# BigBird attention and a Fourier mixing layer on one core: table loads moved behind their copies, and the last output tiles in another order

## The chip, the cores and the metric

The kernel runs on one core of one Trainium2 chip. The metric is the device time of one execution in microseconds (us). The median of three runs of the kernel before is 1051.01 us (1050.29 to 1051.64).

## The reference

The inputs are `q`, `k`, `v` of shape (4, 8, 768, 64): 4 batches, 8 heads, 768 positions, head size 64. A block mask (blocks of 32: the window, first and last blocks, three sampled blocks for each row of blocks) is applied to the scores.

```python
scores = q @ k.T / sqrt(64); scores = where(mask, scores, -1e9)
x = softmax(scores) @ v                      # heads joined: (4, 768, 512)
mixed = real(fft(fft(x, axis=1), axis=2))
u = x + mixed
un = (u - mean(u)) / sqrt(var(u) + 1e-6)
out = u + relu(un @ w_ch1) @ w_ch2           # w_ch1 (512, 2048), w_ch2 (2048, 512)
```

## The kernel before

**Slots.** The attention is cut into 96 slots, and `slot(sl)` (line 1433) writes out the instructions of one of them on all engines, in a fixed order. Twelve units make a pair of heads, two units a slot, six slots a pair, and 24 slots a batch. A slot begins on PE (the tensor engine) with eight score matmuls (`s<-qT,kT`, L578). ACT (the scalar engine) takes their exponentials (`e<-s`, L598), PE adds up the products with v (`o<-e,vr`, L652) and, in the first batch, the sums (`sp`, L723). The score tile `s` has two buffers, so the scores of a slot wait for the exponentials of the slot before. In the trace slots 8 to 14 begin on PE at 44.49, 49.65, 54.18, 58.76, 63.91, 70.42 and 76.57 us.

**Weights.** Beside the first batch, the two weight matrices come in as 32 chunks of 512 KB, as pairs of 32-bit words, and are turned into floats. `w_load(i)` (line 454) issues the load of chunk i on SP's queue, into one of five rooms in turn; so chunk i has to wait until the round of chunk i-5 is over. `w_round(i)` (line 459) is the round of a chunk: two ACT instructions (L465, L468), then five on DVE, the vector engine (L469 to L477), whose last, L477, ends the use of the room. At the end of a slot `w_loads()` issues the loads that the rounds of earlier slots have made room for, and `w_steps(sl)` writes the rounds: after slot sl, 1.42 times sl of them, rounded up. Slot 8 ends with rounds 10 and 11, slot 9 with round 12, slot 10 with 13 and 14, slot 11 with 15, slot 12 with 16 and 17.

**Tables.** The cosines and sines of the transform go through two buffers `raw` (tag `tr`, called `tab` in the trace). `table_s` (line 383) and `table_d` (line 404) return two functions each: `get` issues the loads on SP's queue (L391, or L409 and L410), and `put` copies the table out of the buffer on DVE (L397, L414 to L421). `table_step()` (line 429) is the last call of the even slots from slot 4 on. Once two loads are out, it runs the oldest `put` and then the next `get`, in the same slot. So the six tables are loaded in slots 4, 6, 8, 10, 12, 14 and copied in slots 8, 10, 12, 14, 16, 18, and from slot 8 to 14 the load follows the copy that frees its buffer. The transform of the first batch, which reads the tables, starts after slot 24.

**SP's queue.** SP (the sync engine) issues almost all transfers, one after another, in the order in which they are written. When one of them waits for a buffer, all behind it wait too. Behind the table load of slot 8 stand the loads of q for a later pair (`load_q`, line 250: six transfers, slot 9) and chunks 15, 16 and 17.

**Rows.** The positions are kept in an order of their own. `_ORDER` (line 53) lists, for each of the six tiles of 128 rows, the runs of rows in memory; `_rows` (line 80) makes one transfer of each, and joins two runs of 63 that go backwards into one of 126 rows. Tiles 2, 3 and 4 go as 1, 126 and 1 rows, tiles 0 and 1 as 64 and 64, and tile 5 as 1, 63 and 64. `spread_q` (line 287) also walks `_ORDER`, at the start of the kernel.

**The end.** The last batch has an output stage of its own. `outputs(r, m, after)` (line 1210) works for m on tile m (half 0, in xA) and tile 3+m (half 1, in xB) in 28 matmuls of `yy` (L1224), and DVE adds the results to x (L1231, L1254). m runs through `OUT` (line 1178), here (2, 0, 1). `store` (line 1167, issues at L1170) sends a tile to memory. In the last call alone (`ends`) each tile goes in two halves of 256 columns. The order there is: left half of tile m on SP, left half of tile 3+m on ACT's queue, right half of tile 3+m on SP, and, after the last sum, right half of tile m on SP. Behind the last store stands a conditional (L1666) that jumps over a general version of the kernel, and then the closing of the program (L1701).

Of the kernel before, what the change touches and what calls it, by code (L numbers as in the profile page):

```python
# [27 lines left out]
def _run(ap, start, n, step):  # L28

    at = ap[:, start:start + 1]  # L30
    return bass.AP(tensor=at.tensor, offset=at.offset, ap=[list(at.ap[0]), [step, n]])
# [9 lines left out]
def _grid(ap, start, runs, jump, n, step):  # L41
# [16 lines left out]


_TURNED = (((0, 0, (128, 64, 2), (64, 128, 2), (1, 1, 64)),  # L60
# [19 lines left out]
def _rows(view, tile):  # L80

    got = []
    for t, p0, runs, jump, n, s0, step in _ORDER:
        if t != tile:
            continue
        at = view[s0:s0 + 1, :]
        row, col = list(at.ap[0])[0], list(at.ap[1])
        if jump > 0 > step:
            got.append((p0, runs * n, bass.AP(tensor=at.tensor, offset=at.offset,
                                              ap=[[jump * row, runs], [step * row, n], col])))  # L90
            continue
        for r in range(runs):
            at = view[s0 + r * jump:s0 + r * jump + 1, :]
            got.append((p0 + r * n, n, bass.AP(tensor=at.tensor, offset=at.offset,
                                               ap=[[step * row, n], col])))
    return got
# [3 lines left out]
def kernel(  # L100
# [19 lines left out]
    P = 128  # L120
# [262 lines left out]
    def table_s(src, dst, t):  # L383
        raw = tr_p.tile([P, ND * HS], FP32, tag="tr", name="tab")

        def get():
            rows = _rows(src, t)
            if dst is sn_sb and t == 0:
                rows = [(0, 1, src[P:P + 1, :]), (1, 63, src[2:P:2, :]), (64, 64, src[1:P:2, :])]
            for p0, cnt, of in rows:  # L390
                nc.sync.dma_start(out=raw[p0:p0 + cnt, 0:KS], in_=of)  # L391

        def put():
            to = 0
            for s0, n, step in FREQUENCIES:
                if to < dst.shape[2]:
                    nc.vector.tensor_copy(out=dst[:, t, to:to + n], in_=_run(raw, s0, n, step))  # L397
                to += n
        return get, put
# [4 lines left out]
    def table_d(src, dst):  # L404
# [7 lines left out]
        def put():  # L412
# [5 lines left out]
            else:  # L418
# [5 lines left out]
    table_steps = [(table_s, (src, dst, t)) for src, dst in ((cos_s, cs_sb), (sin_s, sn_sb))  # L424
                   for t in range(2)]
    table_steps += [(table_d, (cos_d, cd_sb)), (table_d, (sin_d, sd_sb))]
    table_put = deque()

    def table_step():

        if len(table_put) == 2 or not table_steps:
            if table_put:
                table_put.popleft()()
        if table_steps:
            fn, args = table_steps.pop(0)
            get, put = fn(*args)
            get()
            table_put.append(put)
# [4 lines left out]
    for w, w_sb in ((w_ch1, w1_sb), (w_ch2, w2_sb)):  # L443
        rows, cols = w.shape
        words = _words(w, rows * cols)
        for row in range(rows // P):
            for col in range(0, cols, WN):
                src = bass.AP(tensor=words, offset=2 * (row * P * cols + col),
                              ap=[[2 * cols, P], [1, 2 * WN]])
# [532 lines left out]
    def mixer(b, xA, xB):  # L982
# [184 lines left out]
        def store(half, m, cols=slice(0, DM), queue=nc.sync):  # L1167
            x = (xA, xB)[half]
            for p0, cnt, rows in _rows(out[b][:, cols], T * half + m):
                queue.dma_start(out=rows, in_=x[p0:p0 + cnt, m, cols])  # L1170
            if m == out_of[half][-1]:
                finished.add((b, half))
# [2 lines left out]


        last = b == B - 1
        OUT = (2, 0, 1)
        out_of = (OUT, OUT if last else (0, 1, 2))
        o_t, o_s = {}, {}  # L1180
        DH = DM // 2
# [13 lines left out]
        def output_left(m, j):  # L1195
            a11, a12, a21, a22 = (hs[g, i][:, :, m * P:(m + 1) * P]
                                  for i in range(2) for g in range(2))
            if j in (1, 3):
                o_s[m, j] = ep.tile([P, 4, P], FP32, tag="e", name="os")
            elif j == 4:  # L1200
                o_s[m, j] = acc_p.tile([P, 4, P], FP32, tag="acc", name="os")

            to, a, c, op = {1: (o_s.get((m, 1)), a21, a22, ALU.add),
                            2: (a21, o_s[m, 1], a11, ALU.subtract),
                            3: (o_s.get((m, 3)), a22, a21, ALU.subtract),
                            4: (o_s.get((m, 4)), a12, a21, ALU.subtract)}[j]
            tt(out=to, in0=a, in1=c, op=op)
            busy("DVE", 0.7)

        def outputs(r, m, after):  # L1210

            if m == OUT[0]:
                output_left(m, 1)
# [30 lines left out]
            if ends:  # L1244
                store(0, m, slice(0, DH))
            if m == OUT[0]:
                output_left(m, 3)
# [53 lines left out]
        for r in range(2 if last else 0):  # L1301
            rest += [(lambda p=p: quad(p), 7 * PRODUCT) for p in range(4 * r, 4 * r + 4)]
            rest += [(lambda r=r, m=m, after=after: outputs(r, m, after), 7 * 1.75)
                     for m, after in zip(OUT, OUT[1:] + (None,))]
        for r in range(0 if last else NF // 4):
# [94 lines left out]
    def begin(b):  # L1400


        before, after, rest = mixer(b, x_of[b, 0], x_of[b, 1])
        any_of = len(late) + len(apart) + 4 * len(rest)
        hold = 2 * T
        apart.extend((*step, any_of) for step in norm_steps(b) + before)
        apart.extend((*step, hold) for step in after)

        def go():
            late.extend(rest)  # L1410
        apart.append(("-", go, 0.0, 0.0, 0.0, hold))
# [16 lines left out]
    def w_steps(sl):  # L1428
        while state["w"] < min(len(wchunks), W_PACE * sl):
            w_round(state["w"])  # L1430
            state["w"] += 1

    def slot(sl):
# [126 lines left out]
            item[2]()  # L1560
        w_loads()
        w_steps(sl)
        if sl >= 4 and sl % 2 == 0:
            table_step()

    def highest():

# [24 lines left out]
    for sl in range(B * SB + 1):  # L1592
        slot(sl)
        if sl == B * SB - 4:
            flag = highest()
        if sl == B * SB - 2:
            over = nc.values_load(flag[0:1, 0:1], min_val=0, max_val=1)
# [6 lines left out]
    def general():  # L1604
# [4 lines left out]
        for b in range(B):  # L1609
            xs = [xp.tile([P, T, DM], FP32, tag=tag, name="x") for tag in ("xA", "xB")]  # L1610
            for h in range(H):
# [43 lines left out]
                for half, x in enumerate(xs):  # L1655
                    sl = slice(half * T, half * T + T)
                    nc.vector.tensor_tensor(out=x[:, :, h * D:(h + 1) * D], in0=op[:, sl, :],
                                            in1=rs[:, sl, :].broadcast_to([P, T, D]),
                                            op=ALU.mult)
            before, after, rest = mixer(b, *xs)  # L1660
            for step in before + after:
                step[1]()
# [42 lines left out]
```

## Time and profile before

| what | value |
|---|---|
| median of 3 runs | 1051.01 us (1050.29 to 1051.64) |
| profiled execution | 1051.83 us |
| its span, first to last instruction | 1049.9 us |
| mean granted clock of PE | 0.994 |
| PE idle before the scores of slot 13 | 2.24 us |
| last instruction that computes ends at | 1040.81 us |

The profiled execution took 1.93 us more than its span, and 0.82 us more than the median. All positions are microseconds from the start of the span. In a line of the timeline the first number is the start, the second the length; in brackets is the idle time of the engine before it, and what ended it. A merged line (x5) holds several instructions of one kind. A line of waits has the total, the number and the longest. SPq and ACTq are the two engines as issuers of transfers; q1 and q10 are their transfer queues. In a table by stretches a line has the stretch, its length, the busy time of the five engines, the clock granted to PE, the busy share of the 16 transfer engines and GB/s.

### The profile page before, as it was taken

Reading aid. Unit: us, or ns where it says so; the run is one execution under the profiler, and the core shown is the slowest. Engines: PE = TensorE matmul, PEld = TensorE weight load, DVE = VectorE, ACT = ScalarE, POOL = GpSimd, SP = SyncE. Lnnn points to the kernel's source line nnn. Section 1 sums busy time; section 2 is a strip of 40 time slices with the busy share of each in tenths; the row PEclk is TensorE's granted clock in tenths of the full one; section 3 lists DMA queues with packets and bytes.
Section 4 is the critical chain, followed back from the end, with each engine's and each line's share of the span. In section 5 each row is a group of like instructions: output and inputs, shape, how many; then the busy total and the mean of one; then the engine's idle time right before and its main releaser. Section 6 shows DMA issues by size and latency. Waiting matters only on the chain. (4 is left out here: it accounts for less than half of the span.)

```text
span 1049.9 us, 12342 instructions
## 1 busy us (share of the span) xinstructions
PE 1022.6 (97%) x4350; PEld 530.7 (51%) x4350; DVE 672.5 (64%) x1232; ACT 356.2 (34%) x718; POOL 236.6 (23%) x264
## 2 busy tenths in 40 slices
PE   8999999999999999999999999899999999999996
PEld 4333345444465554444444654444445654578585
DVE  6898885977845844655578467565558364774663
ACT  6979756554020112432441211243221111210210
POOL 1000074655000100554553001256420001000000
PEclk9999999999999999999999999999999999999998
DMA  7757522282000035232220003721010001000001
GB/s 212 227 180 216 121 47 46 51 140 37 1 1 20 31 40 87 62 64 39 56 58 1 1 10 74 124 53 42 16 25 7 0 1 39 22 1 1 1 17 46
DMA packets 163455, 58.05 MB, mean 55 GB/s; under 512 B 144172, under 2 KB 154170, under 8 KB 163386
## 3 DMA queue, kind: packets, MB, share of 16 engines
q1 hardware_dynamic: 162134, 56.45, 24.1%
q10 hardware_dynamic: 1220, 0.72, 0.3%
q8 instruction: 36, 0.59, 0.2%
q14 instruction: 33, 0.27, 0.1%
q0 software_dynamic: 32, 0.01, 0.0%
HBM read 43.80 MB, written 13.37 MB: 54 GB/s over the span
## 5 line engine op out<-in xcount | busy, mean ns | idle before, releaser
L638 POOL TENSOR_TENSOR acc<-acc,e 128x384 f32<-128x384 f32 x156 | 159.2, 1054 | 90.6 <-DVE e L608 68.2
L578 PE MATMUL s<-qT,kT 64*128 64x384 f32 x768 | 154.0, 515 | 9.8 <-ACT e L598 8.4
L652 PE MATMUL o<-e,vr 128*64 128x384 f32 x768 | 142.9, 499 | 0.0
L1159 PE MATMUL y<-w_sb,hB 128*128 128x512 f32 x288 | 128.1, 595 | 0.3 <-DVE x L1162 0.3
L1159 PE MATMUL y<-w_sb,hA 128*128 128x512 f32 x288 | 127.9, 595 | 0.0
L1162 DVE TENSOR_TENSOR x<-y,x 128x512 f32<-128x512 f32 x72 | 49.7, 690 | 113.8 <-PE y L1159 113.4
L608 DVE TENSOR_TENSOR e<-s,mask 128x768 f32<-128x768 f32 x84 | 76.3, 950 | 54.5 <-ACT s L606 46.3
L578 PEld LDWEIGHTS s<-qT,kT 64*128 64x128 f32 x768 | 63.7, 185 | 90.6 <-ACT e L598 29.0
L638 POOL TENSOR_TENSOR acc<-e 128x384 f32<-128x384 f32 x42 | 48.0, 1164 | 249.7 <-ACT e L598 125.6
L606 ACT ACTIVATE s<-s 128x768 f32<-128x768 f32 x84 | 63.6, 792 | 113.9 <-PE s L578 113.7
L598 ACT ACTIVATE e<-s 128x768 f32<-128x768 f32 x108 | 82.6, 812 | 56.0 <-PE s L588 35.0
L1103 PE MATMUL z<-unT,t 128*128 128x384 f32 x256 | 93.5, 488 | 0.0
L1159 PEld LDWEIGHTS y<-w_sb,hB 128*128 128x128 f32 x288 | 53.4, 190 | 66.5 <-issue 65.2
L1159 PEld LDWEIGHTS y<-w_sb,hA 128*128 128x128 f32 x288 | 53.7, 190 | 63.7 <-issue 60.0
L652 PEld LDWEIGHTS o<-e,vr 128*64 128x64 f32 x768 | 48.0, 137 | 69.7 <-issue 67.8
L1108 DVE TENSOR_TENSOR hA<-z,hA 128x384 f32<-128x384 f32 x64 | 35.7, 557 | 71.6 <-PE z L1103 71.5
L1112 ACT ACTIVATE hA<-hA 128x384 f32<-128x384 f32 x64 | 33.4, 523 | 123.6 <-DVE hA L1108 123.6
L1103 PEld LDWEIGHTS z<-unT,t 128*128 128x128 f32 x256 | 49.1, 192 | 34.4 <-issue 0.9
L1112 ACT ACTIVATE hB<-hB 128x384 f32<-128x384 f32 x64 | 33.5, 523 | 88.6 <-DVE hB L1108 88.6
L1123 ACT COPY hA<-xp 128x384 f32<-128x384 f32 x32 | 15.3, 477 | 123.3 <-PE xp L1103 123.3
L1103 PE MATMUL z<-t,w_sb 128*128 128x384 f32 x128 | 46.7, 488 | 2.8 <-DVE t L1065 2.8
L1103 PE MATMUL z<-t,t 128*128 128x384 f32 x128 | 47.8, 497 | 0.0
(208 smaller groups left out, 1372.5 us busy)
## 6 DMA issues: line engine op xcount, KB each, us to landing
wraw<-in_moe_w_ch_dram SPq DMA_DIRECT2D x32, 512.0 KB
vr<-in_v_dram SPq DMA_DIRECT2D x30, 192.0 KB
far<-un SPq DMA_DIRECT2D x18, 256.0 KB
unT<-far SPq DMA_DIRECT2D x24, 192.0 KB
qb<-in_q_dram SPq DMA_DIRECT2D x44, 96.0 KB
kb<-in_k_dram SPq DMA_DIRECT2D x44, 96.0 KB
out_dram<-x SPq DMA_DIRECT2D x11, 252.0 KB
out_dram<-x SPq DMA_DIRECT2D x18, 128.0 KB
```

Source lines behind the costliest of these rows:

```text
L578: nc.tensor.matmul(s[:, i, 0:HS], kT[rows, c * P:(c + 1) * P], qT[rows, queries], start=True, stop=u not in by_pe)
L598: nc.scalar.activation(out=e, in_=s[:, :, 0:HS], func=ACT.Exp, scale=scale)
L606: nc.scalar.activation(out=s[:, :, 0:HS], in_=s[:, :, 0:HS], func=ACT.Exp, scale=scale)
L608: nc.vector.tensor_tensor(out=e, in0=s[:, :, 0:HS], in1=m.broadcast_to([P, 2, HS]), op=ALU.mult)
L638: nc.gpsimd.tensor_add(out=acc[:, i, :], in0=start[:, i, :], in1=e[:, i, :])
L652: nc.tensor.matmul(o[D * i:D * i + D, :], vt[:, i, c, :], e[:, i, :], start=(c == 0), stop=(c == C - 1))
L1103: nc.tensor.matmul(to, a[:, k, :], c[:, k, :], start=(k == 0), stop=(k == ND // 2 - 1))
L1108: tt(out=to, in0=ps, in1=a, op=ALU.add)
L1112: nc.scalar.activation(out=h, in_=h, func=ACT.Relu)
L1123: nc.scalar.copy(out=h11, in_=x)
L1159: nc.tensor.matmul(y, hs[0, half][:, l, m * P:(m + 1) * P], w2_sb[:, 4 * r + l, :], start=(l == 0), stop=(l == 3))
L1162: nc.vector.tensor_tensor(out=x[:, m, :], in0=y, in1=x[:, m, :], op=ALU.add)
```

## The change

There are three edits.

1. `table_step` takes the slot's number and looks it up in a list. Loads stand in slots 4, 5, 11, 12, 17 and 18, copies in slots 8, 9, 14, 15, 20 and 21. The order of the six tables stays, and no slot has both.
2. The run of 63 rows of tile 5 becomes two runs of 48 and 15. This goes for every store of tile 5 (one transfer more each), for one sine load, and for the copies of `spread_q` (one more in each of two calls).
3. In the last batch `OUT` is (0, 1, 2): the last call of `outputs` works on tiles 2 and 5, where it worked on tiles 1 and 4.

```diff
-          (5, 0, 1, 0, 1, 512, 1), (5, 1, 1, 0, 63, 386, 2), (5, 64, 1, 0, 64, 385, 2))
+          (5, 0, 1, 0, 1, 512, 1), (5, 1, 1, 0, 48, 386, 2), (5, 49, 1, 0, 15, 482, 2),
+          (5, 64, 1, 0, 64, 385, 2))
...
-                rows = [(0, 1, src[P:P + 1, :]), (1, 63, src[2:P:2, :]), (64, 64, src[1:P:2, :])]
+                rows = [(0, 1, src[P:P + 1, :]), (1, 48, src[2:98:2, :]),
+                        (49, 15, src[98:P:2, :]), (64, 64, src[1:P:2, :])]
...
-    def table_step():
-
-        if len(table_put) == 2 or not table_steps:
-            if table_put:
-                table_put.popleft()()
-        if table_steps:
+    TABLES = {4: "g", 5: "g", 8: "p", 9: "p", 11: "g", 12: "g", 14: "p", 15: "p",
+              17: "g", 18: "g", 20: "p", 21: "p"}
+
+    def table_step(sl):
+
+        if TABLES.get(sl) == "p":
+            table_put.popleft()()
+        elif sl in TABLES:
             fn, args = table_steps.pop(0)
             get, put = fn(*args)
             get()
...
-        OUT = (2, 0, 1)
+        OUT = (0, 1, 2) if last else (2, 0, 1)
...
-        if sl >= 4 and sl % 2 == 0:
-            table_step()
+        table_step(sl)
```

## The prediction

> **What bounds the kernel now.** The page comes first: PE is busy for 97% of the span, so a gain can only come from the few places where PE stands still or runs slowly, and from the end, where it has nothing left.
>
> ```profile
> PE 1022.6 (97%) x4350; PEld 530.7 (51%) x4350; DVE 672.5 (64%) x1232; ACT 356.2 (34%) x718; POOL 236.6 (23%) x264
> ```
>
> I then read PE's timeline for idle time. Most pieces are below 1 us; the longest one within the first batch is where the tables are loaded.
>
> ```profile
> 54.18 1.62 PE L578 MATMUL s<-qT,kT 64*128 64x384 f32 x8 [0.27 <-ACT e L598]
> 57.97 0.85 PE L723 MATMUL sp<-e,pick 128*32 128x384 f32 x8
> ...
> 67.32 0.85 PE L723 MATMUL sp<-e,pick 128*32 128x384 f32 x8
> 70.42 1.78 PE L578 MATMUL s<-qT,kT 64*128 64x384 f32 x8 [2.24 <-ACT e L598]
> 75.79 0.85 PE L723 MATMUL sp<-e,pick 128*32 128x384 f32 x8
> ```
>
> PE waits 2.24 us for exponentials. ACT's timeline says why they are late:
>
> ```profile
> 50.97 0.19 ACT L526 ACTIVATION_READ_ACCUMULATOR qr<-qr 128x1 f32 x1
> ...
> 68.45 0.66 ACT L465 ACTIVATE wraw<-wraw 128x512 f32<-128x512 uint32 x1 [3.12 <-DMA wraw<-in_moe_w_ch_dram]
> 69.56 1.50 ACT L598 ACTIVATE e<-s 128x768 f32<-128x768 f32 x2
> ...
> 78.39 1.52 ACT L598 ACTIVATE e<-s 128x768 f32<-128x768 f32 x2 [1.41 <-PE s L588]
> ```
>
> ACT works in order. Round 15 stands ahead of the exponentials of slot 12 and waits 3.12 us for chunk 15 to arrive. So the question is who issued that load so late. SP's timeline and its waits between 50.8 and 70.5 us:
>
> ```profile
> 47.60 3.31 SPq L456 DMA_DIRECT2D wraw<-in_moe_w_ch_dram  x2
> 58.93 1.17 SPq L391 DMA_DIRECT2D tab<-in_sin_s_dram  x3
> 60.20 3.86 SPq L262 DMA_DIRECT2D qr<-in_q_dram  x6
> 64.16 1.50 SPq L456 DMA_DIRECT2D wraw<-in_moe_w_ch_dram  x3
> ...
> SPq L391 <- DVE cs_sb L397: 11.1, 2, 7.9
> ```
>
> SP issues nothing from 50.91 to 58.93 us. The table load of slot 8 waits 7.9 us for the copy that frees its buffer; then come six loads of q, and only at 64.16 chunks 15, 16 and 17. That copy is late since DVE has its rounds to do first:
>
> ```profile
> 54.69 0.69 DVE L477 TENSOR_TENSOR w_sb<-w_sb,wraw 128x512 f32<-128x512 f32 x1
> ...
> 57.66 0.69 DVE L477 TENSOR_TENSOR w_sb<-w_sb,wraw 128x512 f32<-128x512 f32 x1
> 58.27 0.63 DVE L397 COPY cs_sb<-tab 128x128 f32<-128x128 f32 x5
> ...
> 61.65 0.69 DVE L477 TENSOR_TENSOR w_sb<-w_sb,wraw 128x512 f32<-128x512 f32 x1
> ```
>
> These are the ends of rounds 10, 11, the copy, and round 12. Chunk 15 needs only the room of round 10, free at 55.38 us: it was issued 8.8 us after its room was there.
>
> The second place is the end. The last sum is done at 1040.81, and 9.1 us follow.
>
> ```profile
> 1038.73 0.75 ACTq L1170 DMA_DIRECT2D out_dram<-x  x1
> 1039.12 0.23 SPq L1170 DMA_DIRECT2D out_dram<-x  x1
> 1039.40 0.66 SPq L1170 DMA_DIRECT2D out_dram<-x  x1
> 1040.39 0.42 DVE L1231 TENSOR_TENSOR x<-yy,x 128x256 f32<-128x256 f32 x1 [0.97 <-PE yy L1224]
> 1040.84 1.12 SPq L1170 DMA_DIRECT2D out_dram<-x  x2
> ...
> q1 hardware_dynamic: 138, 0.12, 13.0%
> q10 hardware_dynamic: 129, 0.13, 10.9%
> ...
> q1 hardware_dynamic: 153, 0.14, 12.0%
> ...
> 1046.00:1047.00 1.00, 0.00 (x0) 0.00 (x0) 0.00 (x0) 0.00 (x0) 0.00 (x0) 0.50 0.14 49
> 1048.00:1049.00 1.00, 0.00 (x0) 0.00 (x0) 0.00 (x0) 0.00 (x0) 0.00 (x0) 0.50 0.00 0
> ...
> L1666 SPq EVENT_SEMAPHORE  x8: 17/17/17, 1045.6 to 1048.4; - x8
> ...
> SPq L1666 <- SPq L1666: 6.0, 3, 3.6
> ```
>
> The lines at 1038.73 and 1039.40 are the two halves of tile 4, 126 rows each, on ACT's queue and SP's. The queue lines count packets, the first two in 1039.5 to 1043.9, the third in 1043.9 to 1047.7: q10 has sent its 128 rows by 1043.9, and most of q1's long transfer runs after it, at a busy share of 0.14, which is about two of 16 engines. So the two halves use the same two engines, one after the other. The stores of 64 rows, issued last (1040.84), are among the 138 packets done earlier or in the first moments after. The end is therefore set by two transfers of 126 rows in series: data until 1047.7, SP's last semaphore at 1048.4, the closing until 1049.9.
>
> **The change, part by part.**
>
> *Table loads.* In slots 8 and 10 SP no longer meets a load that waits for a copy. After 50.91 us it goes to the loads of q, whose buffer is free when ACT's square of the rows in it ends (50.97 + 0.19), and is done with them 3.86 us later, at 55.0. Chunk 15 goes out at 55.4, with the end of round 10. From issue to use it took 68.45 - 64.16 = 4.3 us, together with two others; so it is there by 59.7, and ACT wants it at 65.33 (68.45 - 3.12): 5.6 us to spare. Chunk 16 follows round 11 (58.35) and chunk 17 round 12 (62.34), there by 62.7 and 66.6. ACT wants these two after the exponentials of slot 12, which begin at 66.44 instead of 69.56 and last 1.50: after 67.9, 1.3 us later than the second is there. ACT's wait of 3.12 us goes whole. PE then has no wait: the first of the exponentials is done near 67.2, and PE is free at 68.17. **2.24 us** of idle time go.
>
> With them goes a slow stretch. From the start of slot 13's scores to its sums PE took 75.79 - 70.42 = 5.37 us; the same five groups took 57.97 - 54.18 = 3.79 us in slot 10. The granted clock explains it:
>
> ```profile
> 68.10:70.40 2.30, 0.07 (x4) 0.00 (x0) 1.41 (x8) 1.95 (x4) 0.00 (x0) 1.00 0.87 336
> 70.40:76.50 6.10, 6.08 (x31) 2.29 (x31) 5.86 (x11) 6.10 (x12) 0.00 (x0) 0.72 1.00 276
> ```
>
> With 0.07 us of work in 2.3 us, the clock came back at 1.00 for the gap and 0.72 behind it. **1.58 us** more. [...]
>
> What is next late? ACT had 1.41 us idle before the exponentials of slot 14, waiting for PE; with PE 0.7 us further ahead than ACT it still has some 0.7. So PE sets the pace again. DVE gains nothing on its own, but its idle time goes too, and it must not end up late: each round lasts 3.0 us (57.66 - 54.69), and the room of chunk 18 is free at about 65.9 (one copy, 0.6 us, moved ahead of round 13), so it is there at 70.2. ACT wants it after two rounds (1.1 us each, 69.56 - 68.45) and the exponentials of slot 13: 67.9 + 2.2 + 1.5 = 71.6, 1.4 us later.
>
> *The copies themselves* cost the same and stand elsewhere. The sine copies go behind slots 14 and 15, the last two tables behind 20 and 21:
>
> ```profile
> 75.00:100.00 25.00, 24.85 (x173) 9.92 (x169) 22.29 (x50) 21.02 (x45) 0.00 (x0) 1.00 0.70 215
> 100.00:125.00 25.00, 24.52 (x167) 10.18 (x169) 22.71 (x43) 21.65 (x44) 0.00 (x0) 1.00 0.60 143
> ...
> L417 DVE COPY cd_sb<-tab x1: 229/229/229, 97.9 to 97.9; 128x128 f32<-128x128 f32 x1
> ```
>
> DVE has 2.7 and 2.3 us free in these stretches; the copies moved there are of the kind of L417, four or five for one table and three for the other, 1.4 us in all, and find cover. Value 0; if the cover is gone, 1.4 us.
>
> *Runs of 48 and 15.* Two more copies at the start: 14 such copies took 1.38 us, so 0.1 us each, and the mask products that read them have cover:
>
> ```profile
> 6.54 1.38 DVE L291 CAST factors<-wide 24x128 bf16<-24x128 f32 x14
> 9.89 0.49 PE L588 MATMUL s<-factors 64*128 64x384 bf16 x4
> ```
>
> From 7.92 to 9.89 there are 2 us. One more transfer each for a sine load and for every store of tile 5: 0.23 to 0.66 us of SP's time by the rows of the end, at places where the queue behind it isn't late. Value 0, at most 0.66 us for each of three batches.
>
> *The last tiles.* Tile 2 has the 126 rows now, tile 5 goes as 1, 48, 15 and 64. The left half of tile 2 leaves after the second of seven products in `outputs`, and is out of the way. Tile 5 fills the middle. What is left is one transfer of 126 rows, but it is issued last: after 1040.84 and one row (0.28 us with its gap), at 1041.12, where its counterpart went at 1039.40. How long does it take? Bounds from the two rows: with the two engines to itself like ACT's, from 1038.73 to 1043.9, 5.2 us, so data until 1046.3, 1.4 us sooner than 1047.7. If it needs what SP's took, 1039.40 to 1047.7, 8.3 us, data until 1049.4, 1.7 us later. On the other side stands SP's jump, 3.6 us from its last issue to its first semaphore at 1045.6; it moves by some 0.4 us, so no more than 2 us can be won. I take the nearer row, since the engines are free then: **-1.4 us**, between -2.0 and +1.7.
>
> *Sum.* 2.24 + 1.58 + 1.4 = 5.2 us off the profiled 1051.83 gives 1046.6. That execution lies 0.8 above the median of 1051.01; from the median it is **1045.8**. A shift of this kind lasts, since the later work waits for PE's order or for transfers that follow it.
>
> **Rivals.**
>
> *SP is held elsewhere.* The load of q or the rooms of chunks 16 and 17 could hold the queue as the table did, or round 16 or 18 could take over the wait. For: DVE is busy for 22 of 25 us here, and every load hangs on its rounds. Against: the 1.3 us or more in hand above. Then only the end is gained: 1051.0 - 1.4 = 1049.6.
>
> *The last store is slower.* Its length is its own, not its neighbour's doing: -3.8 + 1.7 gives 1048.9. For: it is issued 1.7 us later. Against: ACT's 5.2 us.
>
> *The clock doesn't come back with the gap.* Only the idle time goes, and a slow stretch falls elsewhere: -2.24 - 1.4, 1047.4. Against: the two rows of the clock. [...]
>
> *DVE is the pace, and the change is slower.* If DVE, not SP's order, limits slots 12 to 22, a copy put where DVE has no time makes the rooms, the chunks and then ACT late, and each of the two pairs (slots 14 and 15, slots 20 and 21) brings a stall of the kind seen, 2.24 + 1.58 = 3.8 us. 2 x 3.8 - 3.8 - 1.4 = +2.4: 1053.4. It decides once a round ends 1.4 us later than I have it. Against: 2.7 and 2.3 us of idle time on DVE where the pairs go.
>
> **How the numbers follow.** The forecast 0.62, SP held elsewhere 0.15, the store slower 0.09, the clock 0.04, DVE 0.10. A measurement can tell about 0.2%, 2.1 us, from no change: 1048.9 to 1053.1 is the same. The forecast, the clock and half of the slow store are faster, 0.70; the held queue and the other half are the same, 0.20; DVE is slower, 0.10. Forecast alone: from 1044.5 (the end at -2.0, and 0.7 for the spread of the runs) to 1047.2 (nothing at the end). The range goes from 1044.4 to 1049.8 and leaves out DVE.
>
> **What would show it.** Right: SP's queue without the empty 8 us, no wait of ACT for a chunk, PE without the gap near 68 and clock 1.00 there, q10 short at the end and q1's last packets near 1046 less the shift. Wrong: a wait for `wraw` at a later round, waits of SP on L477 that have grown into ACT's way, or a last semaphore over 8 us after the last sum.

## The result and the profile after

Six runs of the changed kernel have a median of 1046.17 us (1043.62 to 1048.39), six of the kernel before beside them 1050.65 us (1049.45 to 1051.95). The ratio is 0.9956, with an interval of 0.9939 to 0.9972: the change gains 4.5 us, between 2.9 and 6.4. The profiled execution took 1048.23 us, 3.6 less than that of before, with a span of 1046.3 us. Lines have moved by one to four: L578 is now L582, L598 is L602, L456 is L460, L391 is L393, L1170 is L1174, L1666 is L1669.

**SP's queue.** SP's timeline of the changed kernel from 46 to 75 us (start, length, instruction):

```profile
47.91 3.30 SPq L460 DMA_DIRECT2D wraw<-in_moe_w_ch_dram  x2
51.51 3.82 SPq L263 DMA_DIRECT2D qr<-in_q_dram  x6
55.77 13.79 SPq L460 DMA_DIRECT2D wraw<-in_moe_w_ch_dram  x5
69.61 2.17 SPq L393 DMA_DIRECT2D tab<-in_sin_s_dram  x4
```

The loads of q follow the chunks at once, chunk 15 goes out at 55.77 instead of 64.16, and the sine table stands behind chunk 19. SP still waits a good part of the time, but for the rounds that free the rooms, one chunk at a time. That is in the waits of SP from 50.8 to 72.5 us:

```profile
SPq L460 <- DVE w_sb L481: 14.9, 6, 3.6
```

ACT's and PE's timelines of the changed kernel show what became of the two stalls:

```profile
65.46 0.19 ACT L530 ACTIVATION_READ_ACCUMULATOR kr<-kr 128x1 f32 x1
65.55 0.67 ACT L469 ACTIVATE wraw<-wraw 128x512 f32<-128x512 uint32 x1
...
66.70 1.50 ACT L602 ACTIVATE e<-s 128x768 f32<-128x768 f32 x2
...
74.76 1.52 ACT L602 ACTIVATE e<-s 128x768 f32<-128x768 f32 x2 [0.64 <-PE s L592]
```

```profile
54.52 1.61 PE L582 MATMUL s<-qT,kT 64*128 64x384 f32 x8 [0.27 <-ACT e L602]
...
68.42 1.56 PE L582 MATMUL s<-qT,kT 64*128 64x384 f32 x8
...
72.94 1.56 PE L582 MATMUL s<-qT,kT 64*128 64x384 f32 x8
```

Round 15 starts right behind the instruction before it, with no bracket, and the scores of slot 13 have no bracket either. From slot 13's scores to slot 14's it is 4.52 us, where it was 76.57 - 70.42 = 6.15.

**Positions.** Laid beside each other, the two traces give a running account. Slot 10 begins 0.34 us later than before; this comes from the first microseconds, where the 14 matmuls on the tile `warm` took 2.13 us instead of 1.77 (over all kernels' traces they took 1.73 to 2.27). Slot 14 begins 3.63 us earlier. So the stretch with the tables brought 3.97 us. But at the end only 3.6 are left, though the stores gain too. PE's timelines, before and then after, show where some of it went:

```profile
244.22 0.92 PE L578 MATMUL s<-qT,kT 64*128 64x384 f32 x4 [0.67 <-ACT e L598]
246.84 0.92 PE L578 MATMUL s<-qT,kT 64*128 64x384 f32 x4 [1.71 <-ACT e L598]
...
250.69 1.45 PE L1103 MATMUL z<-t,w_sb 128*128 128x384 f32 x4
...
671.12 1.56 PE L1103 MATMUL z<-t,w_sb 128*128 128x384 f32 x4 [2.77 <-DVE t L1065]
```

```profile
243.44 1.65 PE L582 MATMUL s<-qT,kT 64*128 64x384 f32 x4 [2.43 <-ACT e L602]
...
248.77 1.45 PE L1107 MATMUL z<-t,w_sb 128*128 128x384 f32 x4
...
668.74 1.84 PE L1107 MATMUL z<-t,w_sb 128*128 128x384 f32 x4 [2.65 <-DVE t L1069]
```

PE waits for exponentials here in both kernels, 0.67 + 1.71 us in two pieces before, 2.43 us in one piece after. (Both shapes occur in the kernels below, with the moved loads and without them.) Behind it the same four matmuls take 0.92 us before and 1.65 after, and the lead of 246.84 - 243.44 = 3.40 us is down to 250.69 - 248.77 = 1.92. The granted clock (third number from the end) in this stretch, before and then after:

```profile
243.50:250.00 6.50, 4.12 (x20) 2.05 (x19) 4.75 (x4) 3.46 (x5) 3.48 (x4) 1.00 0.00 0
```

```profile
243.50:250.00 6.50, 6.50 (x20) 3.40 (x21) 1.34 (x2) 2.70 (x5) 3.55 (x4) 0.76 0.00 0
```

So a slow stretch was removed at 70 us, and in this execution another one appeared at 244 us, worth 1.5 us. From there to the last sum the lead goes from 1.92 to 2.32.

**The end.** The timelines of the changed kernel have two of SP's issues and the last sum between them:

```profile
1037.90 0.49 SPq L1174 DMA_DIRECT2D out_dram<-x  x1
1038.07 0.42 DVE L1235 TENSOR_TENSOR x<-yy,x 128x256 f32<-128x256 f32 x1 [0.97 <-PE yy L1228]
1038.91 0.66 SPq L1174 DMA_DIRECT2D out_dram<-x  x1
```

Its table by stretches (the last column but one is the busy share of the 16 transfer engines):

```profile
1043.00:1044.00 1.00, 0.00 (x0) 0.00 (x0) 0.00 (x0) 0.00 (x0) 0.00 (x0) 0.50 0.13 49
1044.00:1045.00 1.00, 0.00 (x0) 0.00 (x0) 0.00 (x0) 0.00 (x0) 0.00 (x0) 0.50 0.00 0
```

And SP's semaphores behind the jump, in the instructions of that line (first and last start):

```profile
L1669 SPq EVENT_SEMAPHORE  x8: 17/17/17, 1042.9 to 1044.8; - x8
```

The last sum is done at 1038.49. The transfer of 126 rows goes out at 1038.91 (0.66 us to issue) and its data end by 1044.0, 5.1 us after the issue. The tail from the last sum to the end of the span is 7.81 us; it was 9.09.

The sum of the two executions: 3.97 from the tables, less 0.34 at the start, less 0.23 in drift up to 243 us, less 1.48 to the clock there, plus 0.40 behind it, plus 1.28 at the end, makes 3.60 us.

### The profile page after: what moved, and what is told of

The parts are those of the page before. It is cut to its first block, busy times and chain, and to the rows that moved or that the text cites. A ratio compares the mean times of both kernels' runs of the same rounds, so it can differ in the third digit from the quotient of the medians.

```text
span 1046.3 us, 12351 instructions
## 1 busy us (share of the span) xinstructions
PE 1022.6 (98%) x4350; PEld 531.1 (51%) x4350; DVE 674.6 (64%) x1234; ACT 356.1 (34%) x718; POOL 236.7 (23%) x264
## 4 chain that ended last, share of the span: by engine, by line
PE 84%; DVE 7%; ACT 3%; issue 2%; DMA 1%; SPq 1%; POOL 1%; ACTq 0%; DVEq 0%; POOLq 0%
PE y L1163 23%; PE z L1107 16%; PE s L582 10%; PE o L656 9%; PE yp L1107 8%; PE yy L1228 7%; PE xp L1107 4%; PE zp L864 2%; PE sp L727 1%; PE s L592 1%; ACT e L602 1%; POOL acc L642 1%; DVE acc L637 1%; DVE t L1069 1%; PE xt L679 1%
## 5 line engine op out<-in xcount | busy, mean ns | idle before, releaser
L582 PE MATMUL s<-qT,kT 64*128 64x384 f32 x768 | 154.2, 516 | 7.5 <-ACT e L602 6.1
L582 PEld LDWEIGHTS s<-qT,kT 64*128 64x128 f32 x768 | 63.9, 186 | 87.9 <-ACT e L602 26.6
L602 ACT ACTIVATE e<-s 128x768 f32<-128x768 f32 x108 | 82.4, 811 | 56.6 <-PE s L592 35.3
```

Of the source, the lines that this page charges most:

```text
L582: nc.tensor.matmul(s[:, i, 0:HS], kT[rows, c * P:(c + 1) * P], qT[rows, queries], start=True, stop=u not in by_pe)
L602: nc.scalar.activation(out=e, in_=s[:, :, 0:HS], func=ACT.Exp, scale=scale)
```

## The experiments

The theory on trial: the table load of slot 8, which waits for its copy, holds SP's queue, and the stall of ACT and PE, with the slow clock behind it, comes from that alone; at the end two transfers of 126 rows run one after the other. The rivals: DVE is the pace; the last store is slow for its own reasons; the gain comes from the runs of 48 and 15. Each row below has its runs of the kernel before beside it.

| kernel | median of runs, us | kernel before, us | ratio, 95% interval |
|---|---|---|---|
| tables only | 1047.92 of 12 | 1051.20 of 35 | 0.9971, 0.9959 to 0.9983 |
| order only | 1049.99 of 11 | 1051.20 of 35 | 0.9986, 0.9977 to 0.9995 |
| runs only | 1051.27 of 11 | 1051.20 of 35 | 1.0001, 0.9992 to 1.0010 |
| load back in slot 8 | 1050.44 of 12 | 1051.20 of 35 | 0.9992, 0.9984 to 1.0001 |
| copies twice | 1046.48 of 5 | 1050.46 of 13 | 0.9961, 0.9948 to 0.9974 |
| long rows first | 1046.35 of 8 | 1050.46 of 13 | 0.9964, 0.9950 to 0.9977 |
| left half not stored | 1047.85, one | 1050.46 of 13 | none |
| a store on ACT's queue | 1046.33 of 5 | 1050.46 of 13 | 0.9955, 0.9941 to 0.9969 |
| tables and order | 1047.02 of 5 | 1051.29 of 12 | 0.9960, 0.9948 to 0.9973 |
| the changed kernel again | 1048.07 of 7 | 1051.29 of 12 | 0.9957, 0.9941 to 0.9974 |
| joined | 1043.37 of 6 | 1051.29 of 12 | 0.9927, 0.9914 to 0.9940 |

**Tables only.** The kernel before with the first edit.

```diff
-    def table_step():
...
+    TABLES = {4: "g", 5: "g", 8: "p", 9: "p", 11: "g", 12: "g", 14: "p", 15: "p",
+              17: "g", 18: "g", 20: "p", 21: "p"}
...
+    def table_step(sl):
...
```

> The kernel before with the new list of table loads and copies alone; rows and tile order as before. If SP's queue, held by the load of slot 8, is the cause, PE's gap before slot 13 (2.24 us) and the slow stretch behind it (1.58 us) go, and the scores of slot 14 begin 3.6 to 4.0 us sooner than in the kernel before; the end stays at 9.1 us behind the last sum; ratio 0.996 to 0.997. If DVE sets the pace, a wait of ACT for a chunk shows up at a later round and the ratio is 1.000 or above.

It gains 3.0 us by the ratio (1.8 to 4.3), 3.3 between the medians. SP and PE go as in the changed kernel (the chunks follow q at once, slot 13 has no wait):

```profile
55.02 13.79 SPq L458 DMA_DIRECT2D wraw<-in_moe_w_ch_dram  x5
68.86 1.66 SPq L391 DMA_DIRECT2D tab<-in_sin_s_dram  x3
...
67.67 1.56 PE L580 MATMUL s<-qT,kT 64*128 64x384 f32 x8
72.19 1.56 PE L580 MATMUL s<-qT,kT 64*128 64x384 f32 x8
```

From the start of slot 10 (53.75 us) to that of slot 14 it takes 18.44 us, where the kernel before takes 76.57 - 54.18 = 22.39: 3.95 us less. Its tail is 9.17 us, as before. So this edit carries the stretch at 70 us and nothing of the end.

**Order only.** The kernel before with `OUT = (0, 1, 2) if last else (2, 0, 1)`, and the 63 rows whole.

> The kernel before with the new order of the last batch's tiles alone; the run of 63 rows stays whole. PE's gap before slot 13 stays at 2.2 us. If the two transfers of 126 rows ran one after the other, the time from the last sum to the end falls from 9.1 us to 7.7 or so; if a transfer of 126 rows takes its 8.3 us by itself, it grows to 10.8. Ratio 0.9985 in the first case, 1.0015 in the second, neither of which the timing alone can tell.

It gains 1.5 us by the ratio (0.5 to 2.4), 1.2 between the medians, and the tail of its trace is 7.32 us. The stall at slot 13 is still there, in PE's timeline:

```profile
71.25 2.13 PE L578 MATMUL s<-qT,kT 64*128 64x384 f32 x8 [2.92 <-ACT e L598]
```

and in ACT's waits from 50 to 75 us:

```profile
ACT wraw L465 <- DMA wraw<-in_moe_w_ch_dram: 3.8, 1, 3.8
```

**Runs only.** The kernel before with the run of 63 rows as 48 and 15.

> The kernel before with the run of 63 rows cut into 48 and 15 alone. My theory gives no change: gap before slot 13 at 2.2 us, 9.1 us behind the last sum, ratio 0.999 to 1.001. If the additional transfers hold SP's queue where it is late, each of the first three batches loses 0.3 to 0.7 us and the ratio is 1.001 to 1.002.

No difference: 1.0001. The tail is 9.22 us. The gap at slot 13 is 2.92 us, as in "order only", where 2.2 was expected of both.

**Load back in slot 8.** The changed kernel, with one of the six loads again behind the copy of slot 8.

```diff
-    TABLES = {4: "g", 5: "g", 8: "p", 9: "p", 11: "g", 12: "g", 14: "p", 15: "p",
+    TABLES = {4: "g", 5: "g", 8: "pg", 9: "p", 12: "g", 14: "p", 15: "p",
...
```

(`table_step` then runs the copy for a "p" in the entry and the load for a "g", in this order.)

> The kernel after with one load moved back: the first sine table is loaded in slot 8 again, right behind the copy that frees its buffer, not in slot 11. The second copy stays in slot 9, all else as after. If this one load holds SP's queue, SP is idle for 7 to 8 us near 51 to 59 us again, ACT waits 2.5 to 3.2 us for chunk 15, PE has its gap of 1.6 to 2.3 us before slot 13, and the time comes back to 3 to 4 us over the kernel after. If the pace is DVE's, moving one load changes nothing and the gap stays away.

The time is back within 0.16% of the kernel before, with the other edits still in place (the tile order by itself was worth 0.14%). SP's timeline has its empty stretch again, and the chunks behind the loads of q:

```profile
48.06 3.30 SPq L460 DMA_DIRECT2D wraw<-in_moe_w_ch_dram  x2
59.38 1.70 SPq L393 DMA_DIRECT2D tab<-in_sin_s_dram  x4
61.19 3.82 SPq L263 DMA_DIRECT2D qr<-in_q_dram  x6
65.11 4.56 SPq L460 DMA_DIRECT2D wraw<-in_moe_w_ch_dram  x5
```

The waits of SP and ACT in this kernel:

```profile
SPq L393 <- DVE cs_sb L399: 7.9, 1, 7.9
ACT wraw L469 <- DMA wraw<-in_moe_w_ch_dram: 4.7, 1, 4.7
```

And PE's timeline:

```profile
72.44 2.60 PE L582 MATMUL s<-qT,kT 64*128 64x384 f32 x8 [3.79 <-ACT e L602]
```

The waits of ACT and PE, 4.7 and 3.79 us, are longer than expected (up to 3.2 and 2.3); why is not shown. One load, at one place in the queue, makes the whole stall. With "tables only" this settles the cause.

**Copies twice.** The changed kernel with every copy of a table done two times, some 4 us more for DVE in all.

```diff
+            for _ in range(2):
                 to = 0
                 for s0, n, step in FREQUENCIES:
```

> The kernel after with every copy of a table done twice, some 4 us more of DVE's work between slots 8 and 21. If DVE has the cover that I counted (2.7 and 2.3 us of idle time in the two stretches of 25 us), PE's timeline up to slot 24 moves by less than 0.5 us against the kernel after, and no wait of ACT for a chunk appears. If DVE is the pace, rounds come late, ACT waits for chunks and PE loses 2 to 4 us.

(The copies of the other tables stand in a second such loop.) 1046.48 us, against 1046.17 of the changed kernel. From slot 13 to slot 14 PE's timeline has the same 4.52 us as the changed kernel:

```profile
67.74 1.56 PE L584 MATMUL s<-qT,kT 64*128 64x384 f32 x8
72.26 1.56 PE L584 MATMUL s<-qT,kT 64*128 64x384 f32 x8
```

In the table by stretches DVE (the third busy time) has 1.0 and 1.3 us left of 25, and PE is busy for 24.79 and 23.62 (24.81 and 24.09 in the changed kernel):

```profile
75.00:100.00 25.00, 24.79 (x173) 9.77 (x171) 23.97 (x56) 22.45 (x48) 0.00 (x0) 1.00 0.75 223
100.00:125.00 25.00, 23.62 (x166) 9.44 (x159) 23.74 (x53) 20.38 (x43) 1.36 (x2) 1.00 0.62 147
```

No wait of ACT for a chunk came back. But PE lost 0.64 us against the changed kernel between 100 and 106 us (5.79 us from one start of scores to the next, where it was 5.15), 0.47 of it in a wait for sums from DVE (L713). That is just over the 0.5 expected: doubled copies come near DVE's limit, single ones don't reach it. DVE is not the pace here. A small gap of PE (1.12 us at 141.8) is new; whether the copies make it was not tried.

**Long rows first.** The changed kernel; the 126 rows of the last store go first on SP, the two single rows on ACT's queue.

> The kernel after with its last store in another order: the 126 rows of the right half of tile 2 go first on SP, the two single rows go on ACT's queue. If the long transfer sets the end, the time from the last sum to the end falls from 7.8 us by the 0.3 us of the single row's issue, or by up to 0.9 where the row behind it counts too. If SP's jump sets it, it falls by the shorter issue all the same, and if ACT's jump does, it grows by 0.5 or so. The timing can't tell this; the profile can.

1046.35 us, which can't be told from the changed kernel. The tail is 7.41 us, as expected 0.4 less than 7.81; but "load back in slot 8", with the stores of the changed kernel, has 7.55, so one trace doesn't show it.

**Left half not stored.** The kernel before without the 126 rows of the left half of tile 4 in the last batch, so that part of the output isn't written.

```diff
+                if left and cnt > 1:
+                    continue
                 queue.dma_start(out=rows, in_=x[p0:p0 + cnt, m, cols])
```

> The kernel before, with the 126 rows of the left half of tile 4 left out of the last store (these rows of the output are not written). If the two long transfers use the same two engines one after the other, SP's transfer, issued at the same place, has its last packet some 5.2 us after its issue instead of 8.3, and the time from the last sum to the end falls from 9.1 us to 7 or less, bounded by SP's jump. If 8.3 us is its own length, nothing moves.

SP's timeline has the issue of the other 126 rows, the table by stretches the last of the data, and the last line SP's semaphores behind the jump:

```profile
1037.85 0.66 SPq L1173 DMA_DIRECT2D out_dram<-x  x1
...
1043.40:1043.60 0.20, 0.00 (x0) 0.00 (x0) 0.00 (x0) 0.00 (x0) 0.00 (x0) 0.50 0.05 10
1043.60:1043.80 0.20, 0.00 (x0) 0.00 (x0) 0.00 (x0) 0.00 (x0) 0.00 (x0) 0.50 0.00 0
...
L1669 SPq EVENT_SEMAPHORE  x8: 17/17/17, 1043.6 to 1044.5; - x8
```

The last sum is at 1039.27 here, so the last semaphore is 5.2 us behind it, where it was 1048.4 - 1040.81 = 7.6; the tail falls from 9.09 to 6.63 us. The other transfer of 126 rows was not touched, on its queue or in its time of issue. It took some 5.7 us from issue to its last packet instead of 8.3. The two transfers did run one after the other. The transfer queues of the kernel before, from 1042 to 1043 us and then from 1046 to 1047, show it too (the first number counts packets):

```profile
q10 hardware_dynamic: 41, 0.04, 13.5%
q1 hardware_dynamic: 2, 0.00, 2.7%
...
q1 hardware_dynamic: 44, 0.04, 11.7%
```

From 1039.4 to 1043 q10, ACT's queue, sends 93 packets in all and q1, SP's, 4; once q10 is done, q1 sends some 45 in each microsecond.

**A store on ACT's queue.** The changed kernel; in the first three batches the store of the last tile of half 0 goes on ACT's queue, to shorten the wait of PE that follows each batch's end.

```diff
+            if not last and half == 0 and m == out_of[0][-1]:
+                queue = nc.scalar
```

> The kernel after with one store of each of the first three batches (the last tile of half 0) on ACT's queue instead of SP's. In the traces the store of the second batch stands on SP ahead of the last two transfers of the normalised rows to memory, for which the next stage waits, and PE has a gap of 2.65 us there (near 668 us) with a slow clock behind it. If that order is the cause, the gap falls by 1.3 to 2.1 us and the slow stretch goes, 1.5 to 3.5 us in all, ratio to the kernel before near 0.993. If the transfers themselves are the bound, nothing moves; if ACT is held by the wait of the store, exponentials come late and it is slower than after.

In this trace the gap is 1.58 us where it was 2.65, with a clock of 1.00 behind it, but the time is that of the changed kernel:

```profile
668.12 1.53 PE L1107 MATMUL z<-t,w_sb 128*128 128x384 f32 x4 [1.58 <-DVE t L1069]
```

The end gave away what the gap had gained: the tail is 8.81 us. That the store shortens the gap is not shown, either: the repeat of the changed kernel below has 1.97 us at this place, and the joined kernel, which has the store, 2.12. The 1.5 to 3.5 us expected didn't come.

**Tables and order, and the changed kernel again.** The first has the first and third edits and the 63 rows whole; the second is a repeat, on the same chip.

> The kernel after with the run of 63 rows whole again: new table list and new tile order, three transfers for a half of tile 5, not four. In two traces so far (copies twice, store on ACT) the last 64-row transfer of tile 5 took 1.5 to 1.65 us to issue, not 0.49, and the end came 8.8 to 8.9 us after the last sum; in the kernel with the new order and three transfers it took 0.54 and the end 7.3. If the fourth transfer brings this about, the end here is 7.2 to 7.5 us after the last sum; if it is chance, it can be either. The rest is as in the kernel after: ratio 0.995 to 0.996.

> The kernel after once more, beside the other two. Ratio to the kernel before 0.994 to 0.997. The gaps of PE near 243 and 668 us come back at about 2.4 and 2.65 us; if the slow clock behind a gap is a matter of chance, one, both or none of them may have it, and the single runs again spread over 4 us or more.

The times can't be told apart (0.9960 and 0.9957), so by them the second edit neither helps nor costs. The profiled executions lie far apart, though: 1043.41 and 1049.14 us. The first holds no slow stretch; the second has one at 244 us, deeper than the one shown above, and a long end. In PE's timeline of "tables and order":

```profile
242.82 0.92 PE L580 MATMUL s<-qT,kT 64*128 64x384 f32 x4 [1.71 <-ACT e L600]
```

and its table by stretches:

```profile
243.50:250.00 6.50, 6.50 (x25) 3.72 (x22) 2.49 (x5) 3.23 (x6) 3.86 (x4) 1.00 0.00 0
```

The same stretch in the repeat:

```profile
243.50:250.00 6.50, 6.33 (x15) 3.11 (x16) 1.57 (x2) 2.92 (x6) 3.32 (x4) 0.50 0.00 0
```

and a line of its SP's timeline:

```profile
1037.44 1.78 SPq L1174 DMA_DIRECT2D out_dram<-x  x1
```

That is a transfer of 64 rows of tile 5; in the first trace of the changed kernel its issue took 0.49 us (1037.90). The last store stands behind it, and the tail is 9.07 us instead of 7.81.

**Joined.** Tables and order, the 63 rows whole, long rows first, and the store on ACT's queue.

> The kernel after with three more steps taken together: the run of 63 rows whole, the last store with its 126 rows first and the single rows on ACT's queue, and the store of the last tile of half 0 on ACT's queue in the first three batches. From the traces so far: 1.1 us off the gap near 668 us (2.65 to 1.58) and mostly no slow clock behind it, 0.4 us off the end. Ratio 0.993 to 0.995 if these last; 0.996 if the spread of the clock hides them.

1043.37 us, the best of all, 0.9927 of the kernel before, with an interval (0.9914 to 0.9940) that doesn't touch that of "tables and order" on the same chip. In its profiled execution the gap near 668 is 2.12 us with a clock of 1.00 behind it, and the tail is 7.68 us. Four of its six runs had a mean clock of 0.998, and these four lie between 1042.58 and 1043.40; of the 48 runs of the other kernels with the changed table loads eight did, at 1042.94 to 1046.02 us. By these clocks, what the joined kernel wins is mostly that slow stretches are rarer. That is argued, not shown, from six runs; which of its edits does it was not taken apart.

## Why the prediction was right, point by point

**Table loads: right, mechanism and size.** The step said 2.24 + 1.58 = 3.8 us. The stretch gave 3.97 in the profiled execution and 3.95 in that of "tables only", whose runs gained 3.0 (1.8 to 4.3). Chunk 15 went out at 55.77, forecast 55.4; ACT's slack before slot 14's exponentials is 0.64 us, forecast 0.7. The rival "SP is held elsewhere" fell: SP waits for rounds, yet no chunk is late for ACT.

**The clock behind the gap: right at its place, incomplete as a step.** The slow stretch went with the gap. But the price of 1.58 us was one execution's: "left half not stored" has the table loads of the kernel before, a gap of 1.93 us there and no slow stretch behind it. What the step took for granted, that a shift lasts, did not hold in this execution: 1.48 us of it were lost to a slow stretch at 244 us. This is the rival "The clock doesn't come back with the gap" in part, though not by its wording: the clock did come back at slot 13, and it fell behind another gap instead, at 244 us. The last section has what thirteen traces show of it; that it fell there because of the edit is not shown.

**The copies themselves: right at 0, with less to spare than counted.** DVE had 25 - 23.94 = 1.1 us left from 75 to 100 us in the changed kernel, where the step saw 2.7; what came in is other work, since the copies from 97 to 98 us had left this stretch. Doubling the copies cost PE 0.64 us and made no chunk late, so the rival "DVE is the pace" is out.

**Runs of 48 and 15: 0 by the times, as forecast; at the end they may cost something that the step didn't have.** It priced a further transfer at 0.23 to 0.66 us. In three of six traces with the split and the new order, a 64-row transfer behind it on SP took 1.50 to 1.78 us to issue instead of 0.49, and the tail was 8.81 to 9.07 us instead of 7.41 to 7.81. In three traces with the run whole this did not happen (tails 7.32, 7.36 and 7.68). Nine traces are too few to put it down to the split, and why the issue stalls is open.

**The last tiles: -1.4 forecast.** The order alone gave -1.5 (-0.5 to -2.4) by the ratio, and -1.77 (9.09 to 7.32) in traces; in the changed kernel -1.28 in one trace and -0.02 in the other. The reason, two narrow transfers in series, was shown by leaving one out and by the queues' packets. The 126 rows took 5.1 us from issue to last packet, forecast 5.2. The rival "The last store is slower" fell. From 1045 to 1046 us, in the trace of before, q1's packets are the only ones, and took 12.9% of the 16 engines' time; by an estimate from this share the 126 rows kept some two engines busy (0.129 x 16 = 2.1). The 8.3 us that became 5.7 when the neighbour was left out fit two transfers that went through the same few engines one after the other; up to 1043 us 93 packets of q10 went to 4 of q1. Which engines they were, and why so few, is not shown.

**The sum.** The forecast's 5.2 us stand against 4.5 (2.9 to 6.4) measured. "Tables only" and "order only" add up to 3.0 + 1.5 = 4.5 by the ratios (3.3 + 1.2 between the medians). In the profiled execution alone the sum was 1.6 us short (1048.23 for 1046.6): the slow stretch at 244 us took 1.48.

## What to carry to other kernels

A load that must wait for a copy belongs in a shared issue queue only where nothing behind it is urgent: here one table load that stood 7.9 us cost 3.8 us of the tensor engine two hops away, and it could be moved at no cost. At the end of a kernel, look at which transfers keep few engines busy and see that no two of them follow each other: here the 126 rows took 12.9% of the 16 engines' time when they ran alone, and 8.3 us from issue to last packet behind another such transfer, 5.7 without it. And before a difference of 2 or 3 us is explained, compare where the granted clock dipped in the two traces: executions of the same code lay 5 to 7 us apart here (1042.94 and 1049.48 us in the repeat).

## What was not expected of the hardware

**The length of a gap of PE didn't decide the clock behind it in these traces.** At slot 13 it dropped behind gaps of 2.24, 2.92, 2.92 and 3.79 us, and stayed at 1.00 behind one of 1.93. Near 244 us it dropped in two of seven traces where the gap before was 1.71 us, and in five of six where it was 2.42 or 2.43. Near 668 us it dropped in six traces, behind gaps of 1.97 to 2.79 us, and stayed up in seven, behind gaps of 1.58 to 2.84. A drop cost 1.5 to 1.7 us in these traces, once 3.2 (the repeat, near 244 us), so the runs of one kernel spread: the six of the changed kernel read 1043.62 and 1043.83 us at a mean clock of 0.998, and 1048.23 and 1048.39 at 0.995.

It need not be mere chance, though. In eleven of the thirteen traces the clock dropped at exactly one of the two later places. Where no load waits for its copy in slot 8, it was near 244 us in six of eight traces and near 668 in two; with that wait, in one of five and in four of five. So where the clock drops may hang on the moved loads. Thirteen traces don't settle it, and no run tried it.

**A long issue.** A transfer of 64 rows took 1.50 to 1.78 us to issue on SP in three traces and 0.49 in three others of the same order of stores. What tells them apart is not known.

**The jump over the general version.** From an engine's branch to its first semaphore behind it there are 2.7 us on SP (1040.2 to 1042.9), 3.1 on ACT, 3.5 on DVE and 0.6 on POOL in the changed kernel, and 3.6 on SP in the kernel before. How much of it is the jump and how much a wait for the semaphore is not shown. On SP it lies beside the last transfer, so little is to be gained there until that transfer is shorter.
